# A third buffer for the first layer's raw weights, and one buffer fewer in two other places

## The chip, the cores and the metric

One core of a Trainium2 chip runs one program. A core has TensorE (PE; its weight loads are listed as PEld), VectorE (DVE), ScalarE (ACT), GpSimd (POOL) and SyncE (SP), which run their own instruction streams in order and wait for each other by semaphores, and 16 DMA engines that move data between the off-chip memory (HBM) and the on-chip memory (SBUF, 128 partitions). The metric is the device time of one execution in microseconds (us).

## The reference

Two residual branches, each behind a layer norm that a conditioning vector shifts and scales. 2048 tokens of 576 channels.

```python
sa, ca, ga, sb, cb, gb = ...            # (silu(c) @ w_mod), six vectors of 576
h = layernorm(x) * (1 + ca) + sa
x = x + ga * A(h)
h = layernorm(x) * (1 + cb) + sb
x = x + gb * B(h)

def A(u):                               # a long convolution over the tokens, per channel
    dt = exp(log_dt)
    P = exp((-exp(log_A_real) + 1j * A_imag) * dt * pos)      # 576 x 128 x 2048
    K = 2 * einsum("dn,dnl->dl", C * dt, P).real              # the kernel, 576 x 2048
    y = irfft(rfft(K, 4096) * rfft(u, 4096))[:2048]
    return y + u * D_skip

def B(x):                               # 576 -> 4608 -> 576
    return relu(x @ w1) @ w2
```

All data is float32.

## The kernel before

**The token blocks.** The 2048 tokens are worked in NB = 4 blocks of 512. For block s the convolution `conv(s)` makes the block's new x, its second layer norm and, by transposes, the operand tiles xh, xl and xs of the two-layer net; then 36 groups (NF = 36) of 128 hidden channels run for that block in `ffn`. So g counts 144 groups, block g // 36. To keep float32 accuracy with the rounded type that TensorE multiplies fast, each operand is split into a high and a low part; a product is made of three matmuls (high x high, high x low, low x high).

**One group of the net.** `first(g)` is 14 matmuls of w1's tile with xh, xl and xs into the PSUM tile hps (line 1326). ScalarE makes hh = relu(hps) (line 1331), DVE the low part hl (line 1332). `second(g)` is 14 matmuls of hh and hl with w2's tile into five accumulators (line 1352). In program order `second(g-1)` stands after `first(g)`.

**Where its weights come from.** The raw tiles are r1 (128 x 640, of w1, 320 KB) and r2 (128 x 576, of w2, 288 KB); both have the program's name r in the profile. They are loaded from HBM by SyncE's queue (lines 1271 and 1275), with two buffers for r1 and three for r2, and asked for three groups ahead: `load_r1(g + 3)`, `load_r2(g + 3)` at the head of group g's turn. ScalarE copies them to the rounded high part (`hi1`, line 1291; `hi2`, line 1301). In block 0 DVE subtracts to get the low parts (`lo1`, line 1296; `lo2`, lines 1307 and 1308), and SyncE's queue stores these to HBM (L1d, L2d, line 1408); in blocks 1 to 3 they are loaded back from there (lines 1280 and 1311), so r1 is then free again after the copy of line 1291. In block 0 it is free after the subtraction of line 1296. The tiles w1 and w2 have three buffers each. In the turn of group g, program order is: the loads, the stores of low parts, `first(g)`, `hi2(g+1)` and `lo2(g+1)`, `hi1(g+2)` and `lo1(g+2)`, `low1(g+3)`, `second(g-1)`.

**What runs between.** While the 36 groups of block b run, a generator does the work of the next block piece by piece: `step(g)` takes pieces until the block's rate is met (it counts the estimated DVE time that each piece yields). In block 0 this is `KGen.rest` for 12 sets of 48 channels (h), which makes the convolution kernel of later blocks, and then `conv(1)`. In block 1 it is the output of block 0 (`finish(0)`), `rest` again for h = 6 to 11, and `conv(2)`; in block 2 `finish(1)` and `conv(3)`; in block 3 `finish(2)`. What is left of a generator at the end of its block runs before the next block starts.

**`rest`.** For each h the tiles W0 (768 KB), Z (96 KB) and W2 (1536 KB) are loaded by POOL's queue, in program order (line 47 is the helper that keeps it; the tiles appear as W, Zr and W2r). A rotation (`rot`, lines 481 to 487) is four DVE operations; in block 1 the first of h reads W0 and makes the first half of W1, the second reads that half. `products` (line 515) multiplies W2 and W1 on TensorE, and ScalarE copies the result out (line 525). W0 and Z have three buffers, W2 two. The loads of W0 and Z for the second next h stand at the head of h's turn, that of W2 for the next h at its end.

**The convolution.** `product` multiplies spectra on DVE: a product into the tile T (line 1030), then a sum or difference with it (line 1032). T comes from `half`: two buffers in block 0's own convolution (ns = 6), three in those of blocks 1 to 3 (ns = 7).

**What sets the order.** A list scheduler orders the instructions of each engine by the program's order and by its own estimates of when things are ready; instructions wrapped in `Kept` or `keep_in_program_order` stay in program order. A tile that takes a buffer waits for the buffer's last readers. Pools are opened on two sides of SBUF, and the pools of the convolutions and of `rest` reuse each other's space one after the other.

Of the kernel before, what the change touches and what calls it, by code (L numbers as in the profile page):

```python
# [10 lines left out]
F32 = mybir.dt.float32  # L11
# [7 lines left out]
P = 128  # L19
# [8 lines left out]
H = 48  # L28
NH = 12
PC = 288  # L30
# [19 lines left out]
class KGen:  # L50
# [10 lines left out]
    def v(self, out, a, b, op):  # L61
        self.tc.keep_in_program_order(self.nc.vector.tensor_tensor(out, a, b, op=op))  # L62
# [391 lines left out]
    def rest(self, psum, plan):  # L454

        nc, k = self.nc, self.k
        v = nc.vector.tensor_tensor
        hs = list(plan)
        with ExitStack() as ctx:
            pt = k.pool(ctx, f"kr{len(hs)}", side="right")  # L460
            d = Kept(k.tc, nc.gpsimd).dma_start

            def load0(h):
                W0 = pt.tile([P, 2, H, 16], F32, tag="W0", bufs=3, name=f"W0_{h}")
                Z = pt.tile([P, 2, 2, H], F32, tag="Z", bufs=3, name=f"Zr_{h}")
                d(out=W0.rearrange("p r c a -> p (r c a)"), in_=k.W1d[h])
                d(out=Z.rearrange("p i r c -> p (i r c)"), in_=k.Zd[h])
                return W0, Z

            def load2(h):  # L470
                W2 = pt.tile([P, 2, H, 32], F32, tag="W2", bufs=2, name=f"W2r_{h}")
                d(out=W2.rearrange("p r c b -> p (r c b)"), in_=k.W2d[h])
                return W2

            def rot(out, X, Z, i):
                T = pt.tile([P, 2, H, 16], F32, tag="T", name="T")
                zr, zi = (
                    Z[:, i, r].unsqueeze(1).unsqueeze(3).broadcast_to([P, 2, H, 16])
                    for r in range(2)
                )  # L480
                v(T, X, zi, op=ALU.mult)  # L481
                yield 1.75
                v(out, X, zr, op=ALU.mult)  # L483
                yield 1.75
                v(out[:, 0], out[:, 0], T[:, 1], op=ALU.subtract)  # L485
                yield 0.95
                v(out[:, 1], out[:, 1], T[:, 0], op=ALU.add)  # L487
                yield 0.95

            def rots(h, W1, W0, Z):  # L490
                blocks = plan[h]
                a = [W1[:, :, :, 16 * i : 16 * i + 16] for i in range(len(blocks))]
                if blocks[0] == 1:
                    yield from rot(a[0], W0, Z, 0)
                    if len(blocks) > 1:
                        yield from rot(a[1], W0, Z, 1)
                        yield from rot(a[2], a[0], Z, 1)
                else:
                    yield from rot(a[0], W0, Z, 1)
                    yield from rot(a[1], a[0], Z, 0)  # L500

            ke = {}

            def products(h, W1, W2):
                blocks = plan[h]
                na = 16 * len(blocks)
                if h % 6 == 0:
                    ke[h // 6] = pt.tile([P, na, 72], F32, tag=f"ke{na}", bufs=1, name=f"ker_{h}")
                for half in range(2):
                    ps = psum.tile([P, 6, na], F32, tag="cps", bufs=1, name="kps")  # L510
                    for q in range(6):
                        for dd in range(4):
                            ch = dd * 12 + 6 * half + q
                            for r in range(2):
                                nc.tensor.matmul(  # L515
                                    ps[32 * dd : 32 * dd + 32, q, :],
                                    W2[:, r, ch],
                                    W1[:, r, ch],
                                    start=(r == 0),
                                    stop=(r == 1),  # L520
                                )
                        if q == 2:
                            yield None
                    q0 = 12 * (h % 6) + 6 * half
                    nc.scalar.activation(  # L525
                        ke[h // 6][:, :, q0 : q0 + 6], ps.rearrange("p q a -> p a q"), AF.Copy
                    )
                    yield None
                if h % 6 == 5:
                    yield -1  # L530
                    for i, s in enumerate(blocks):
                        self.store(
                            s, h // 6, ke[h // 6][:, 16 * i : 16 * i + 16].rearrange("p a q -> p (a q)"),
                            nc.sync,
                        )

            nxt = [load0(hs[0])]
            W2 = load2(hs[0])
            nxt.append(load0(hs[1]))
            for _ in range(1 if len(hs) == NH else 7):  # L540
                yield -1
            prev = iter(())
            for i, h in enumerate(hs):
                W0, Z = nxt.pop(0)
                if i + 2 < len(hs):
                    nxt.append(load0(hs[i + 2]))
                na = 16 * len(plan[h])
                bufs = 1 if len(plan[h]) != len(plan[hs[i - 1]]) else 2
                W1 = pt.tile([P, 2, H, na], F32, tag=f"W1{na}", bufs=bufs, name=f"W1r_{h}")
                yield from spread(rots(h, W1, W0, Z), prev, len(plan[h]))  # L550
                prev = products(h, W1, W2)
                if i + 1 < len(hs):
                    W2 = load2(hs[i + 1])
            yield from prev


def spread(a, b, n):

    for i, w in enumerate(a):
        yield w  # L560
        if i % n == n - 1:
            yield next(b, 0.0)
    yield from b


class Body:
# [259 lines left out]
        return self.cv.tile([P, 4, 2, PC], F32, tag="S", bufs=self.ns, name=name)  # L826

    def half(self, name):
        return self.cvl.tile([P, 4, PC], F32, tag="T", bufs=self.ns - 4, name=name)

    def load(self, src, name):
        t = self.spec(name)
# [426 lines left out]
    def ffn(self, gens):  # L1259

        nc, I, ff = self.nc, self.I, self.ff
        n = NB * NF
        r1, r2, w1, w2 = {}, {}, {}, {}
        late = []

        def queue(g):
            return Kept(self.tc, nc.sync) if g < 2 else nc.sync

        def load_r1(g):
            r1[g] = ff.tile([P, 5, P], F32, tag="r1", bufs=2, name="r1")  # L1270
            queue(g).dma_start(out=r1[g], in_=I["w1"][g % NF])

        def load_r2(g):
            r2[g] = ff.tile([P, D], F32, tag="r2", bufs=3, name="r2")
            queue(g + 1).dma_start(out=r2[g], in_=I["w2"][(g % NF) * P : (g % NF) * P + P, :])
# [14 lines left out]
        def hi1(g):  # L1290
            copy(g - 1)(w1[g][:, 0], r1[g], AF.Copy)  # L1291
# [7 lines left out]
        def hi2(g):  # L1299
            w = w2[g] = ff.tile([P, 1152], F32R, tag="w2", bufs=3, name="w2")  # L1300
            copy(g)(w[:, 0:D], r2[g], AF.Copy)  # L1301

        def lo2(g):
            w, r = w2[g], r2.pop(g)
            if g < NF:
                v = vec(g)
                v(w[:, D:640], r[:, 512:D], w[:, 512:D], op=ALU.subtract)
                v(w[:, 640:], r[:, :512], w[:, :512], op=ALU.subtract)
                late.append((self.L2d[g], w[:, D:]))
            else:  # L1310
                nc.sync.dma_start(out=w[:, D:].bitcast(F32), in_=self.L2d[g % NF])
# [84 lines left out]
        yield  # L1396
        load_r2(1)
        load_r1(2)
        load_r2(2)
        prev = None  # L1400
        for g in range(n + 1):
            if g < n:
                if g + 3 < n:
                    load_r1(g + 3)
                if g + 3 < n:
                    load_r2(g + 3)
                for dst, src in late:
                    nc.sync.dma_start(out=dst, in_=src.bitcast(F32))
                late.clear()
                new = (g, *first(g))  # L1410
                if g + 1 < n:
                    hi2(g + 1)
                    lo2(g + 1)
                if g + 2 < n:
                    hi1(g + 2)
                    lo1(g + 2)
                if g + 3 < n:
                    low1(g + 3)
                step(g)
            if prev is not None:  # L1420
                second(*prev)
                if prev[0] % NF == NF - 1:
                    self.evacuate(prev[0] // NF)
            if g < n:
                prev = new
                step(g)
                if g % NF == NF - 1:
                    for _ in gens[g // NF]:
                        pass
                    done[0] = 0.0  # L1430
# [126 lines left out]
```

## Time and profile before

| | us |
|---|---|
| median of 3 runs (1337.91 to 1348.62) | 1338.05 |
| the profiled execution | 1346.28 |
| its span, first to last instruction | 1344.5 |
| PE busy | 1218.3 (91%) |
| DVE busy | 895.8 (67%) |
| ACT busy | 494.6 (37%) |
| mean granted TensorE clock | 0.934 |
| DMA, mean over the span | 257 GB/s |

Busy times are sums over the span; a matmul's end is modelled, so a busy PE is not PE at its peak. A row of a group reads: line, engine, operation, out<-in, size, count, then busy us and mean ns of one, then the engine's idle time just before these instructions and what ended most of it. A row in order of time reads: start in us, length in us, engine, line, operation, out<-in, and in brackets the idle time before it and what ended that. A row of the waits reads: who waited for whom, us in total, times, the longest. A row of a window reads: stretch and its length, the busy time (and count) of PE, PEld, DVE, ACT and POOL, the granted clock, the share of the DMA engines, GB/s.

### The profile page before, as it was taken

The numbers are of one execution on the slowest core, as the hardware profiler recorded it, in microseconds if no ns is written. First come the engines' busy times: TensorE is split into PE (matmuls) and PEld (weight loads), VectorE is DVE, ScalarE is ACT, GpSimd is POOL, SyncE is SP. The second block draws the span as 40 slices with busy tenths as digits, with TensorE's granted clock in tenths as the row PEclk, the third lists the DMA queues.
The fourth block names the chain that finished last, engine by engine and source line by source line (L and its number), as shares of the span: only waits on it lengthen the run. The fifth ranks groups of instructions, "written<-read, shape, count | busy, mean of one in ns | idle before, by whom it ended". The sixth has DMA issues, their size and how long they took to land.

```text
span 1344.5 us, 26011 instructions
## 1 busy us (share of the span) xinstructions
PE 1218.3 (91%) x10720; PEld 963.8 (72%) x10720; DVE 895.8 (67%) x1324; ACT 494.6 (37%) x863; POOL 162.5 (12%) x260
## 2 busy tenths in 40 slices
PE   4565686889989998999999999999999999999997
PEld 3344564667768676777777887887888888888885
DVE  5999978997995999768658995467996221111112
ACT  5688523222223422622234225433323352323331
POOL 0656501001100100011001000100000000000000
PEclk9556767999999998999999999999999999999998
DMA  8567972987878877698889995867996667666661
GB/s 269 218 231 291 307 272 80 346 298 273 320 279 288 297 247 290 206 400 322 281 276 339 346 357 160 275 219 271 349 392 189 176 178 230 193 197 199 199 177 53
DMA packets 122379, 345.85 MB, mean 257 GB/s; under 512 B 23916, under 2 KB 24212, under 8 KB 111508
## 3 DMA queue, kind: packets, MB, share of 16 engines
q1 hardware_dynamic: 105364, 226.96, 50.9%
q0 software_dynamic: 16384, 115.85, 23.0%
q8 instruction: 84, 1.38, 0.4%
q10 hardware_dynamic: 512, 1.38, 0.3%
q14 instruction: 35, 0.29, 0.1%
HBM read 262.73 MB, written 81.40 MB: 256 GB/s over the span
## 4 chain that ended last, share of the span: by engine, by line
PE 72%; DVE 14%; DMA 7%; issue 4%; ACT 2%; POOL 1%; ACTq 0%; POOLq 0%; DVEq 0%; SPq 0%
PE acc L1352 29%; PE hps L1326 28%; DMA r<-in_w_dram 4%; PE ps_f L846 4%; PE kps L71 2%; PE ph L71 2%; PE kps L515 2%; PE ps_i L1053 2%; DVE W1r L483 2%; DVE T L481 2%; DMA L2d<-w 1%; DVE W1r L487 1%; DVE W1r L485 1%; DVE T L62 1%; DVE w L1296 1%
## 5 line engine op out<-in xcount | busy, mean ns | idle before, releaser
L1326 PE MATMUL hps<-xh,w 128*128 128x512 f32 x1152 | 393.6, 402 | 1.9 <-issue 1.1
L1352 PE MATMUL acc<-w,hh 128*128 128x512 f32 x1152 | 370.6, 403 | 12.9 <-ACT hh L1331 12.9
L1332 DVE SCALAR_TENSOR_TENSOR hl<-hps,hh 128x512 fp32r<-128x512 f32 x144 | 99.1, 688 | 310.1 <-ACT hh L1331 309.3
L1352 PEld LDWEIGHTS acc<-w,hh 128*128 128x128 f32 x1152 | 216.3, 189 | 60.7 <-ACT hh L1331 14.5
L1326 PEld LDWEIGHTS hps<-xh,w 128*128 128x128 f32 x1152 | 218.5, 190 | 50.2 <-issue 1.6
L1326 PE MATMUL hps<-xl,w 128*128 128x512 f32 x576 | 229.7, 400 | 0.1
L1352 PE MATMUL acc<-w,hl 128*128 128x512 f32 x576 | 223.0, 399 | 0.9 <-DVE hl L1332 0.9
L1331 ACT ACTIVATE hh<-hps 128x512 fp32r<-128x512 f32 x144 | 85.8, 596 | 289.7 <-PE hps L1326 289.4
L1301 ACT ACTIVATE w<-r 128x576 fp32r<-128x576 f32 x141 | 96.7, 686 | 231.0 <-PE acc L1352 219.5
L1291 ACT ACTIVATE w<-r 128x640 fp32r<-128x640 f32 x140 | 102.7, 733 | 92.8 <-DMA r<-in_w_dram 92.8
L1326 PEld LDWEIGHTS hps<-xl,w 128*128 128x128 f32 x576 | 109.3, 190 | 23.9 <-DVE xl L47 0.6
L1352 PEld LDWEIGHTS acc<-w,hl 128*128 128x128 f32 x576 | 107.9, 189 | 24.7 <-DVE hl L1332 2.1
L1326 PE MATMUL hps<-xs,w 128*128 128x512 f32 x288 | 98.6, 413 | 0.0
L71 PE MATMUL kps<-W,W 128*32 128x16 f32 x2304 | 39.9, 211 | 45.3 <-POOL W L68 28.1
L1032 DVE TENSOR_TENSOR Y<-Y,T 128x1152 f32<-128x1152 f32 x60 | 79.4, 1351 | 0.0
L71 PEld LDWEIGHTS kps<-W,W 128*32 128x32 f32 x2304 | 35.1, 144 | 59.0 <-POOL W L68 30.8
L847 ACT ACTIVATE Z<-ps_f 128x288 f32<-128x288 f32 x120 | 48.8, 408 | 70.2 <-PE ps_f L846 68.8
L515 PEld LDWEIGHTS kps<-W1r,W2r 128*32 128x32 f32 x3456 | 44.7, 113 | 37.7 <-issue 19.0
L515 PE MATMUL kps<-W1r,W2r 128*32 128x48 f32 (+2 forms) x3456 | 52.1, 201 | 14.6 <-ACT ker L525 9.3
L1471 POOL DMA_DIRECT2D out_dram<-x x16 | 8.7, 544 | 468.6 <-DVE x L1463 466.3
L1326 PEld LDWEIGHTS hps<-xs,w 128*128 128x128 f32 x288 | 54.0, 191 | 11.3
L1352 PE MATMUL acc<-hl,w 128*128 128x512 f32 x144 | 56.7, 394 | 0.0
(235 smaller groups left out, 1586.6 us busy)
## 6 DMA issues: line engine op xcount, KB each, us to landing
r<-in_w_dram SPq DMA_DIRECT2D x144, 320.0 KB, 7.3
r<-in_w_dram SPq DMA_DIRECT2D x144, 288.0 KB, 5.1
w<-L1d SPq DMA_DIRECT2D x108, 320.0 KB, 3.2
w<-L2d SPq DMA_DIRECT2D x108, 288.0 KB, 2.8
W2r<-W2d POOLq DMA_DIRECT2D x18, 1536.0 KB, 9.2
W2d<-W SPq DMA_DIRECT2D x12, 1536.0 KB, 8.6
Ua<-Ud POOLq DMA_DIRECT2D x15, 1152.0 KB, 9.6
W<-W1d POOLq DMA_DIRECT2D x18, 768.0 KB, 10.6
```

Of the source, the lines that this page charges most:

```text
L71: self.tc.keep_in_program_order(self.nc.tensor.matmul(*args, **kw))
L481: v(T, X, zi, op=ALU.mult)
L515: nc.tensor.matmul(ps[32 * dd : 32 * dd + 32, q, :], W2[:, r, ch], W1[:, r, ch], start=(r == 0), stop=(r == 1),)
L846: nc.tensor.matmul(o, fc[:, n2, c, :], src(n2), start=True, stop=True)
L847: ev = nc.scalar.activation(Z[:, n2, c], ps[:, :PC], AF.Copy)
L1032: v(y, y, T, op=op or ALU.add)
L1291: copy(g - 1)(w1[g][:, 0], r1[g], AF.Copy)
L1301: copy(g)(w[:, 0:D], r2[g], AF.Copy)
L1326: nc.tensor.matmul(ps, a, x, start=(i == 0), stop=(i == 13))
L1331: nc.scalar.activation(hh, ps, AF.Relu)
L1332: nc.vector.scalar_tensor_tensor(hl, ps, 0.0, hh, op0=ALU.max, op1=ALU.subtract)
L1352: nc.tensor.matmul(acc[i], a, x, start=(f == 0 and seen[i] == 1), stop=(f == NF - 1 and seen[i] == (3 if i < 4 else 2)),)
```

## The change

Three things:

- r1 gets a third buffer, and is asked for four groups ahead: `load_r1(3)` is added ahead of the loop, and in the loop `load_r1(g + 4)` takes the place of `load_r1(g + 3)`. r2 stays as it is.
- T has two buffers in all convolutions (three before in those of blocks 1 to 3).
- In block 1's `rest`, W0 has two buffers instead of three, and W0 and Z of h + 2 are asked for after the first rotation of h (`ahead`), in place of the head of h's turn. Block 0's `rest` keeps its three buffers and its place for the loads.

```diff
@@ KGen.rest
         hs = list(plan)
+        whole = len(hs) == NH
...
-                W0 = pt.tile([P, 2, H, 16], F32, tag="W0", bufs=3, name=f"W0_{h}")
+                W0 = pt.tile([P, 2, H, 16], F32, tag="W0", bufs=2 + whole, name=f"W0_{h}")
...
                     yield from rot(a[0], W0, Z, 1)
+                    ahead(h)
                     yield from rot(a[1], a[0], Z, 0)
...
+            def ahead(h):
+                if h + 2 in plan:
+                    nxt.append(load0(h + 2))
...
-            for _ in range(1 if len(hs) == NH else 7):
+            for _ in range(1 if whole else 7):
...
-                if i + 2 < len(hs):
+                if whole and i + 2 < NH:
                     nxt.append(load0(hs[i + 2]))
@@ Body.half
-        return self.cvl.tile([P, 4, PC], F32, tag="T", bufs=self.ns - 4, name=name)
+        return self.cvl.tile([P, 4, PC], F32, tag="T", bufs=2, name=name)
@@ Body.ffn
-            r1[g] = ff.tile([P, 5, P], F32, tag="r1", bufs=2, name="r1")
+            r1[g] = ff.tile([P, 5, P], F32, tag="r1", bufs=3, name="r1")
...
         load_r2(2)
+        load_r1(3)
         prev = None
         for g in range(n + 1):
             if g < n:
-                if g + 3 < n:
-                    load_r1(g + 3)
+                if g + 4 < n:
+                    load_r1(g + 4)
                 if g + 3 < n:
                     load_r2(g + 3)
```

## The prediction

> **What bounds the kernel now.** I read the page first: span, then the chain that ended last.
>
> ```profile
> span 1344.5 us, 26011 instructions
> PE 72%; DVE 14%; DMA 7%; issue 4%; ACT 2%; POOL 1%; ACTq 0%; POOLq 0%; DVEq 0%; SPq 0%
> L1291 ACT ACTIVATE w<-r 128x640 fp32r<-128x640 f32 x140 | 102.7, 733 | 92.8 <-DMA r<-in_w_dram 92.8
> ```
>
> TensorE carries 72% of the chain, and one row of the groups names what the change is about: the copy L1291, which makes the first layer's high half from the raw tile r1, left ScalarE idle for 92.8 us waiting for r1 to land. Whether that costs time depends on where it happens, so next the windows, cut near the changes of token block (block 0 from 236, where its first group is through, to 561; then 789 and 1011):
>
> ```profile
> 236.00:561.00 325.00, 299.39 (x3383) 230.82 (x3382) 284.82 (x381) 96.33 (x183) 24.64 (x44) 0.96 0.80 289
> 561.00:789.00 228.00, 224.09 (x2047) 177.08 (x2047) 174.77 (x209) 76.38 (x145) 24.83 (x43) 1.00 0.89 326
> 789.00:1011.00 222.00, 222.00 (x975) 179.49 (x974) 166.04 (x230) 84.65 (x155) 12.35 (x22) 1.00 0.79 277
> 1011.00:1344.50 333.50, 323.58 (x1442) 267.08 (x1440) 70.87 (x117) 105.83 (x171) 4.32 (x8) 0.99 0.61 179
> ```
>
> The columns are length, busy time of PE, weight loads, DVE, ACT and POOL, granted clock, DMA share and GB/s. From 561 on PE is busy in all but 14 us of 783: no load can be worth much there. Block 0 is the loose one: PE is idle for 25.6 us of 325 and DVE for 40.2, so both are nearly full and either can be the limit. Then the waits inside block 0, with those of SyncE's own queue behind them:
>
> ```profile
> ACT w L1291 <- DMA r<-in_w_dram: 82.6, 19, 11.2
> PE acc L1352 <- ACT hh L1331: 12.9, 3, 6.2
> PE kps L515 <- ACT ker L525: 5.3, 1, 5.3
> SPq L1275 <- DVE w L1308: 191.2, 27, 14.0
> SPq L1271 <- DVE w L1296: 14.8, 28, 3.4
> ```
>
> 82.6 of the 92.8 us lie here. How it reaches PE is seen in one stall in order of time:
>
> ```profile
> 277.09 0.33 SPq L1271 DMA_DIRECT2D r<-in_w_dram  x1
> 287.57 0.75 SPq L1271 DMA_DIRECT2D r<-in_w_dram  x1
> 297.51 0.74 ACT L1291 ACTIVATE w<-r 128x640 fp32r<-128x640 f32 x1 [8.82 <-DMA r<-in_w_dram]
> 298.16 0.24 ACT L525 ACTIVATE ker<-kps 128x96 f32<-128x96 f32 x1
> 298.45 0.48 PE L515 MATMUL kps<-W1r,W2r 128*32 128x16 f32 x18 [5.34 <-ACT ker L525]
> ```
>
> ScalarE works in order. The copy of group 9 waits 8.82 us for a tile asked for at 287.57; behind it stand the small copy L525 and the relu L1331, and PE needs one of these. The other stalls of PE that end with work queued behind that copy:
>
> ```profile
> 248.12 0.71 PE L1352 MATMUL acc<-w,hh 128*128 128x512 f32 x1 [2.14 <-ACT hh L1331]
> 401.28 0.79 PE L1352 MATMUL acc<-w,hh 128*128 128x512 f32 x1 [6.19 <-ACT hh L1331]
> 526.45 0.80 PE L1352 MATMUL acc<-w,hh 128*128 128x512 f32 x1 [4.53 <-ACT hh L1331]
> 604.24 0.56 PE L515 MATMUL kps<-W1r,W2r 128*32 128x32 f32 x36 [2.68 <-ACT ker L525]
> ```
>
> With the 5.34 above that is 20.9 us of idle PE, 18.2 of it in block 0. After four of them the clock is down:
>
> ```profile
> 248.20:251.60 3.40, 3.40 (x8) 2.65 (x9) 3.40 (x3) 0.69 (x1) 0.00 (x0) 0.50 0.97 401
> 298.45:302.80 4.35, 4.35 (x56) 3.60 (x57) 4.35 (x6) 0.43 (x1) 0.00 (x0) 0.50 0.90 353
> 401.28:405.20 3.92, 3.92 (x98) 3.05 (x99) 3.87 (x6) 1.05 (x3) 0.00 (x0) 0.50 0.08 29
> 526.45:531.50 5.05, 5.05 (x12) 3.99 (x13) 5.05 (x7) 1.25 (x2) 0.00 (x0) 0.50 0.11 45
> ```
>
> At clock 0.50 half of each stretch is lost: 1.7, 2.2, 2.0 and 2.5, together 8.4 us. PE's own loss to the wait is therefore 20.9 + 8.4 = 29.3 us. [...]
>
> **Third buffer for r1.** Before, r1(g+3) takes the tile of r1(g+1); after, r1(g+4) does. The event that frees it is the same (the subtraction L1296 of g+1 in block 0, the copy L1291 of g+1 later), so the request for each tile goes out where now the one before it goes out, and SyncE's queue keeps its shape: the SyncE rows show that L1275 (r2) waits long for L1308, and L1271 then only 0.5 us more. For group 9 the request moves from 287.57 to 277.09, 10.5 us against a wait of 8.82. The longest wait of all is 11.2, so I take nearly all of the 82.6 us as gone. One request of 320 KB moves out of the loop to ahead of it: at block 0's 289 GB/s that is 1.1 us of transfer. Bounds 0 to 1.1 us; I take nothing, since the loop's first copies have their tiles by then.
>
> What the stalls are worth is not PE's loss alone, because DVE is the limit in much of block 0. First its busy time (third pair of columns) over 123 us of it, then the waits of DVE that follow the stalls:
>
> ```profile
> 263.00:386.00 123.00, 112.30 (x2075) 86.88 (x2076) 115.83 (x123) 28.09 (x52) 12.63 (x24) 0.96 0.82 295
> ```
>
> ```profile
> 260.91 1.76 DVE L483 TENSOR_TENSOR W1r<-W,Zr 128x1536 f32<-128x1536 f32 x1 [2.43 <-PE kps L515]
> 322.92 1.76 DVE L483 TENSOR_TENSOR W1r<-W,Zr 128x1536 f32<-128x1536 f32 x1 [7.17 <-PE kps L515]
> 401.25 0.69 DVE L1332 SCALAR_TENSOR_TENSOR hl<-hps,hh 128x512 fp32r<-128x512 f32 x1 [2.51 <-ACT hh L1331]
> 410.61 0.69 DVE L1332 SCALAR_TENSOR_TENSOR hl<-hps,hh 128x512 fp32r<-128x512 f32 x1 [5.46 <-ACT hh L1331]
> 522.64 1.36 DVE L1030 TENSOR_TENSOR T<-Ka,Ua 128x1152 f32<-128x1152 f32 x1 [0.97 <-DMA Ua<-Ud]
> 543.96 0.46 DVE L1058 TENSOR_TENSOR x<-ps_i,x 128x288 f32<-128x288 f32 x1 [1.44 <-PE ps_i L1053]
> ```
>
> In those 123 us DVE is idle for 7.2, which is the wait of 7.17 at 322.92 and nothing else. For each stall I take the smaller of PE's loss and of DVE's wait that comes of it. First stall: PE 2.14 + 1.7 = 3.8, DVE 2.43: 2.4. Second: PE 5.34 + 2.2 = 7.5, DVE 7.17: 7.2. Third: PE 6.19 + 2.0 = 8.2, DVE 2.51 + 5.46 = 8.0: 8.0. Fourth: PE 4.53 + 2.5 = 7.0, DVE 0.97 + 1.44 = 2.4: 2.4. In block 1, where DVE has room, PE's 2.68: 2.7. Sum 22.7 us. Where the wait goes, the next late thing is the tile after it, which now has the old tile's place in the queue: it lands just when it is wanted, and that is why I take the smaller side each time.
>
> **Two product tiles (T).** The product L1030 and the sum L1032 that reads it are both on DVE, which works in order, so a tile fewer adds no wait on another engine; it can only force a sum to stand directly behind its own product. The nearest row for that is in the chain:
>
> ```profile
> 484.66 0.31 issue
> ```
>
> It is time in front of a sum L1032 for which nothing is named. A gain is out, since a buffer fewer lets nothing start earlier. The convolution in block 0 has 12 such pairs (2 and 4, for two halves): 0 to 12 x 0.31 = 3.7 us. I take the middle, 1.9. In blocks 1 and 2 DVE has 53 and 56 us of room and it costs nothing.
>
> **Two W0 tiles in block 1.** W0 of h+2 is now asked for when the first rotation of h has read W0 of h, no longer at the start of h, and its request stands in POOL's queue ahead of W2 of h+1.
>
> ```profile
> 576.35 0.53 POOL L47 DMA_DIRECT2D W<-W1d  x1 [1.50 <-DMA out_dram<-x]
> 584.38 1.75 DVE L483 TENSOR_TENSOR W1r<-W,Zr 128x1536 f32<-128x1536 f32 x1
> 605.42 1.76 DVE L481 TENSOR_TENSOR T<-W,Zr 128x1536 f32<-128x1536 f32 x1
> DMA to landing us min/median/max: 9.4/12.8/16.1
> 609.36 0.53 POOL L47 DMA_DIRECT2D W2r<-W2d  x1 [16.46 <-PE kps L515]
> ```
>
> The third W0 (h = 8) moves from 576.35 to 586.1, when L483 of h = 6 has read its tile; with the slowest landing of that stretch, 16.1, it is there at 602.2, and its first reader L481 is at 605.42. So 3.2 us are left over, and 2.7 for the small Z tile that goes out right behind it, one issue of 0.53 later. W2 of h = 7 now stands behind both, until 587.2, and at 16.1 again lands by 603.3; its products come after those of h = 6, which end at 609.36. Cost nothing, hidden by the rotations of h = 7; if that cover is gone DVE starts a rotation a few us late, and DVE has 53 us of room in this block. Bounds 0 to 3 us.
>
> **The sum.** 22.7 - 1.9 = 20.8 us off the profiled execution of 1346.3 us (span 1344.5 and 1.8 around it), 1325.5. That execution lies 8.2 us above the median of the runs shown, 1338.05, and inside their spread (1337.91 to 1348.62). I take the same difference off the median: 1317.
>
> **Rivals.** *PE gets it all:* the scheduler lets DVE work slide into the freed places, and the whole 29.3 us come back: 1309. For it: DVE idles 40.2 us in block 0. Against: the 123 us shown above, in which DVE has no idle time but the one wait.
>
> *The next wait takes over:* the following r1 tile, the stores of the low halves and DVE's own load eat half or more of it. For it: DVE is busy 284.8 of 325 us, so in a block 0 shortened by 20 us it would be at 93%; and each next tile lands when the stalled one did, so a group that runs earlier can find it late in its turn. Then a third to a half of 22.7 remains, 7 to 11 us: 1327 to 1331, about 1329.
>
> *The tiles land no earlier:* if the DMA engines were full, asking earlier would only move the waiting into the queue: 1338. For it: shares of 0.97 and 0.90 in two of the slow stretches. Against: 0.80 over block 0, and 0.08 and 0.11 right behind the other two stalls, when nothing was asked for. [...]
>
> *Slower, by ScalarE's order:* with r1 there a group earlier, the list scheduler puts the copy L1291 in front of the relu of the same group also in blocks 1 and 2, where it now stands behind it:
>
> ```profile
> 740.21 0.60 ACT L1331 ACTIVATE hh<-hps 128x512 fp32r<-128x512 f32 x1 [2.49 <-PE hps L1326]
> 740.70 0.73 ACT L1291 ACTIVATE w<-r 128x640 fp32r<-128x640 f32 x1
> ```
>
> Each of these 72 groups would get its relu up to 0.73 us late, 52.6 us at most. It makes the kernel over 1% slower once 20.8 + 13.4 = 34.2 us of that are really lost, that is 47 of 72 groups in full; all of them give 1338 - 20.8 + 52.6 = 1370. Against: what lets L1291 go at 740.70 is the same end of the first layer that lets the relu go, since the w1 tile has three buffers and not r1; and there is room before PE needs the relu.
>
> **How the numbers follow.** Forecast 0.46, with its own range from 1311 (the fourth stall at PE's 7.0 instead of 2.4 and no cost of T: 27.3) to 1323 (T at 3.7, W0 at 3, the extra request at 1.1: 14.9); PE gets it all 0.08; next wait takes over 0.26; no earlier landing 0.07; slower 0.13. The likeliest is the forecast, 1317. The range takes in all but the slower case: from 1308, the whole of PE's loss, to 1340, no gain and the 1.9 us of T. That holds 0.87; without the case of no gain it would hold exactly 0.80 and end at 1331, which leaves the take-over case no room for the upper ends of the costs, so I leave it in. About 1% (13.4 us) is what a measurement of this kernel can tell from no change. Faster by more: 0.46 + 0.08 = 0.54; within: 0.26 + 0.07 = 0.33; slower: 0.13.
>
> **What would show it.** In the profile after: L1291's idle time on r1 under 15 us; the stalls of PE behind ScalarE in block 0 gone, and with them most of the stretches at clock 0.50; block 0 some 300 to 306 us long, DVE busy over 93% of it; blocks 1 to 3 unchanged to 3 us; in block 1 no DVE wait on W0. I am wrong if r1's wait is gone and block 0 stays above 318 us: then DVE or another transfer was the limit all along. I am wrong in the mechanism if r1's wait stays.

## The result, and the profile after

The kernel after takes 1332.58 us (median of 20 runs, 1329.04 to 1340.35), the kernel before, run beside it on the same chips, 1342.51 us (20 runs, 1337.91 to 1351.3). The ratio is 0.9932, with a 95% interval from 0.9916 to 0.9947: 0.7% or about 9 us faster, where 20.8 us (1.6%) were forecast. It is inside the 1% that was called no change. The profiled execution has a span of 1331.4 us, against 1344.5 before. Of these 13.1 us, 8.6 lie in block 0 and 2.1 in block 1; the other 2.5 lie ahead of group 0, whose start varies from 223.3 to 229.1 us over all profiles of this document.

From the page of the kernel after, its span and the row of the copy of the first layer's high half (L1291 before, L1297 now):

```profile
span 1331.4 us, 25993 instructions
L1297 ACT ACTIVATE w<-r 128x640 fp32r<-128x640 f32 x140 | 102.6, 733 | 59.1 <-DMA L1d<-w 53.8
```

The wait for r1 is gone to the last microsecond. In its place the same copy waits 53.8 us for something else: the landing of `L1d<-w`, the store of the low half of a w1 tile. That tile has three buffers; the copy of group g+3 writes into the one whose low half group g has stored, and may not start before the store has read it. Next, the waits within block 0 (from the first matmul of group 0 to that of group 36, 224.80 to 548.70; columns: us in total, times, longest), and above them the row of the window:

```profile
224.80:548.70 323.90, 304.02 (x3404) 233.98 (x3405) 291.92 (x393) 100.00 (x189) 27.83 (x50) 0.97 0.81 291
ACT w L1297 <- DMA L1d<-w: 53.8, 11, 11.3
PE kps L517 <- ACT ker L527: 8.1, 3, 4.7
PE kps L517 <- issue: 5.7, 5, 2.0
PE acc L1358 <- ACT hh L1337: 3.2, 2, 2.8
DVE hl L1338 <- ACT hh L1337: 20.0, 9, 8.3
SPq L1281 <- DVE w L1314: 178.4, 26, 12.0
```

The same cut of the kernel before:

```profile
227.30:559.80 332.50, 306.78 (x3405) 236.62 (x3406) 292.16 (x393) 100.25 (x189) 27.79 (x50) 0.95 0.79 283
PE acc L1352 <- ACT hh L1331: 12.9, 3, 6.2
PE kps L515 <- ACT ker L525: 5.3, 1, 5.3
PE kps L515 <- issue: 5.0, 4, 2.4
```

Block 0 went from 332.5 to 323.9 us. It was forecast at 300 to 306 for a slightly different cut of 325.0, that is 19 to 25 us shorter, where the terms of the sum that lie in block 0 give 18.1. Taken off that cut, the 8.6 us leave about 316, just under the 318 that was named as the sign of being wrong. TensorE's stalls behind ScalarE (the PE rows that name ACT) went from 18.2 to 11.3 us, not to nothing. Ahead of each of the four of over 1 us (1.61, 1.79, 4.70 and 2.77) the copy has just waited for that store, 2.9, 2.7, 7.0 and 11.3 us. One of them, in order of time:

```profile
378.09 0.33 SPq L1277 DMA_DIRECT2D r<-in_w_dram  x1
378.48 0.96 SPq L1415 DMA_DIRECT2D L2d<-w  x1
379.49 1.77 SPq L1415 DMA_DIRECT2D L1d<-w  x1
...
393.29 0.74 ACT L1297 ACTIVATE w<-r 128x640 fp32r<-128x640 f32 x1 [6.99 <-DMA L1d<-w]
394.50 0.41 ACT L527 ACTIVATE ker<-kps 128x288 f32<-128x288 f32 x1
...
394.96 1.29 PE L517 MATMUL kps<-W1r,W2r 128*32 128x48 f32 x52 [4.70 <-ACT ker L527]
```

The store's way from issue to landing in this stretch:

```profile
DMA to landing us min/median/max: 13.7/13.7/13.7
```

So the store of 379.49 landed at 393.2, and the copy of three groups later started at 393.29. The stall comes at nearly the same place as that of 401.28 in the kernel before, and is 4.70 instead of 6.19 us long. There the copy for group 19 held up the relu; here the copy for group 20 holds up the second layer's copy and the small copy L527. The clock still falls at four places in block 0, for 17.0 us together instead of 31.1:

```profile
394.00:400.80 6.80, 5.84 (x105) 4.81 (x105) 0.09 (x1) 1.34 (x4) 0.00 (x0) 0.50 0.33 131
516.90:520.30 3.40, 3.40 (x10) 2.66 (x9) 3.40 (x4) 1.31 (x2) 0.00 (x0) 0.50 0.38 146
281.30:284.70 3.40, 3.40 (x100) 2.53 (x92) 3.40 (x6) 1.17 (x2) 0.00 (x0) 0.51 0.00 1
346.20:349.60 3.40, 3.05 (x19) 2.48 (x19) 3.40 (x5) 0.00 (x0) 0.00 (x0) 0.50 1.01 317
```

### The profile page after: what moved, and what is told of

It is laid out like the page before. It is cut to its first block, busy times and chain, and to the rows that moved or that the text cites. A ratio compares the mean times of both kernels' runs of the same rounds, so it can differ in the third digit from the quotient of the medians.

```text
span 1331.4 us, 25993 instructions
## 1 busy us (share of the span) xinstructions
PE 1209.0 (91%) x10720; PEld 956.7 (72%) x10720; DVE 895.4 (67%) x1324; ACT 494.5 (37%) x863; POOL 162.8 (12%) x260
## 3 DMA queue, kind: packets, MB, share of 16 engines
q0 software_dynamic: 16384, 115.85, 23.1%
q8 instruction: 84, 1.38, 0.4%
q10 hardware_dynamic: 512, 1.38, 0.3%
## 4 chain that ended last, share of the span: by engine, by line
PE 68%; DVE 17%; DMA 7%; issue 4%; ACT 2%; POOL 1%; SPq 0%; ACTq 0%; DVEq 0%; POOLq 0%
PE acc L1358 28%; PE hps L1332 27%; PE ps_f L852 5%; DMA L1d<-w 3%; PE kps L71 2%; PE ph L71 2%; DVE T L482 2%; DVE W1r L484 2%; PE ps_i L1059 2%; PE kps L517 1%; DVE w L1302 1%; DVE W1r L486 1%; DVE W1r L488 1%; DVE w L1314 1%; DVE T L62 1%
## 5 line engine op out<-in xcount | busy, mean ns | idle before, releaser
L1358 PE MATMUL acc<-w,hh 128*128 128x512 f32 x1152 | 366.4, 400 | 3.3 <-ACT hh L1337 3.2
L1297 ACT ACTIVATE w<-r 128x640 fp32r<-128x640 f32 x140 | 102.6, 733 | 59.1 <-DMA L1d<-w 53.8
L853 ACT ACTIVATE Z<-ps_f 128x288 f32<-128x288 f32 x120 | 49.0, 410 | 70.5 <-PE ps_f L852 68.5
L1358 PE MATMUL acc<-hh,w 128*128 128x512 f32 x144 | 57.5, 399 | 0.0
```

What stands on the lines that cost most here:

```text
L853: ev = nc.scalar.activation(Z[:, n2, c], ps[:, :PC], AF.Copy)
L1358: nc.tensor.matmul(acc[i], a, x, start=(f == 0 and seen[i] == 1), stop=(f == NF - 1 and seen[i] == (3 if i < 4 else 2)),)
```

## The experiments

Three theories of where the other 11 us are. The *store theory* (S in the first expectations): the store's landing now holds the copy, and takes back most of what r1's wait cost. The *order theory* (O): what counts is that a waiting copy stands ahead of the relu on ScalarE. The *VectorE theory* (V): block 0 is set by VectorE, so TensorE's stalls were never worth what they last. Three more came up on the way: full DMA engines (traffic), the supply of TensorE's instructions, and TensorE's own work as the limit.

**The small tiles alone.** The kernel after with r1 at two buffers, asked for three groups ahead, as before:

```
-            r1[g] = ff.tile([P, 5, P], F32, tag="r1", bufs=3, name="r1")
+            r1[g] = ff.tile([P, 5, P], F32, tag="r1", bufs=2, name="r1")
-        load_r1(3)
-                if g + 4 < n:
-                    load_r1(g + 4)
+                if g + 3 < n:
+                    load_r1(g + 3)
```

> The changed kernel with r1 back at two buffers and three groups ahead: only the two smaller pools (T, W0) are left of the change. Theory S (the store of a w1 tile's low half now limits the copy L1297), theory O (the relu stands behind a waiting copy on ScalarE, whatever the copy waits for) and theory V (VectorE is the limit of block 0) all expect the time of the kernel before, ratio 0.997 to 1.003, with the copy's wait for r1 again at 85 to 100 us. If the smaller pools cost what the prediction allowed them (up to 3.7 + 3 us) the ratio is 1.002 to 1.005; then the third buffer alone would be worth more than the whole change shows.

Measured: ratio 0.9987, interval 0.9961 to 1.0014. The two smaller tiles cost nothing that can be seen, and the gain is r1's. The order of the instructions on each engine is that of the kernel before, and yet the copy's wait for r1 in block 0 is 60.9 us and not 82.6: so much does this wait differ between two executions of one order.

```profile
ACT w L1297 <- DMA r<-in_w_dram: 60.9, 16, 11.4
```

**The tile w1 in two parts,** three buffers for its high half and four for its low half, so that the copy no longer waits for the store:

```
-            w = w1[g] = ff.tile([P, 2, 5, P], F32R, tag="w1", bufs=3, name="w1")
+            w = w1[g] = [ff.tile([P, 5, P], F32R, tag=f"w1{x}", bufs=dict(h=3, l=4)[x], name="w1") for x in "hl"]
```

> The changed kernel with the w1 tile as two tiles, the high half with three buffers and the low half with four, so that the copy into the high half need not wait until the low half's store has landed. Theory S: the copy's wait for the store (53.8 us) falls under 10 us, the two stalls of PE behind ScalarE in block 0 go, ratio to the kernel before 0.983 to 0.988 (the change alone: 0.993). Theory V: the wait falls as well, but block 0 gets shorter by at most 3 us, ratio 0.990 to 0.994. Theory O: like S, as long as nothing else takes the copy's wait.

Measured: 0.9979 (0.9953 to 1.0005), slower than the kernel after. The store's wait is gone, but two others stand in its place:

```profile
ACT w L1297 <- PE hps L1332: 54.1, 19, 7.4
ACT w L1297 <- DMA r<-in_w_dram: 36.3, 6, 10.2
PE kps L517 <- issue: 13.5, 6, 3.2
PE acc L1358 <- ACT hh L1337: 8.7, 3, 4.3
```

The expectation of the store theory missed. The edit was no clean test, since r1 came late again; why it did is open.

**ScalarE in the written order,** all through block 0, on the kernel after and on the one before:

```
-            return (Kept(self.tc, nc.scalar) if g < 3 else nc.scalar).activation
+            return (Kept(self.tc, nc.scalar) if g < NF else nc.scalar).activation
-            nc.scalar.activation(hh, ps, AF.Relu)
+            copy(g)(hh, ps, AF.Relu)
```

> The changed kernel with the relu and the two copies of each group of block 0 held in program order on ScalarE, so that the relu of group g stands ahead of the copies for groups g+1 and g+2; buffers and loads as in the changed kernel. Theory O: the copy still waits for the store (30 us or more in all), but no PE stall behind ScalarE of over 1.5 us is left in block 0, ratio 0.983 to 0.989. Theory S: the first layer of group g+2 waits for its tile instead of the second layer waiting for its relu, ratio 0.991 to 0.995. Theory V: 0.990 to 0.995.

> The kernel before, with two buffers for r1, and the same order held on ScalarE in block 0. Theory O: the wait for r1 stays (60 us or more) but costs PE little, ratio 0.986 to 0.993, as good as the change or better. Theory S and the prediction's own step (the tile's landing is what costs the time): ratio 0.997 to 1.002, since every tile lands as late as before.

Measured: 1.0052 (1.0021 to 1.0084) and 1.0079 (1.0064 to 1.0094), both slower than before. And yet the copies hardly wait any more: on the kernel after not at all for the store, on the kernel before 5.8 us in block 0 for raw tiles, with two buffers for r1. That was in no expectation, and it shows that a wait of ScalarE is not yet time. On the kernel after, group 20 starts at 406.4 us instead of 413.2; but groups 20 to 24 take 50.0 us instead of 36.1 and groups 32 to 36 45.7 instead of 36.1. In the first of these two stretches TensorE waits 4.0 us for the convolution's copies (L853), where the kernel after has no such wait, and the clock is 0.90 instead of 1.00. That these copies then stand behind the layer's is the likely reason, not shown by itself. So the order was kept for groups 0 to 18 alone (`g < 19` in the lines above), and the stores were tried ahead of the loads in SyncE's queue, each alone and both together:

```
             if g < n:
+                for dst, src in late:
+                    nc.sync.dma_start(out=dst, in_=src.bitcast(F32))
+                late.clear()
                 if g + 4 < n:
                     load_r1(g + 4)
                 if g + 3 < n:
                     load_r2(g + 3)
-                for dst, src in late:
-                    nc.sync.dma_start(out=dst, in_=src.bitcast(F32))
-                late.clear()
```

> The kernel after, with the stores of the two low halves put in SyncE's queue ahead of the two loads of the group instead of behind them; TensorE's order is the same to the instruction, and the other engines' nearly so. Store theory (the first layer's copy now waits for the landing of the low half's store, and this wait is what ate the forecast gain): the copy's wait for the store falls from 53.8 us to under 20, the TensorE stalls at 395 (4.70 us) and 516 (2.77 us) go, and the time is about 8 us below the kernel after: ratio to before 0.987. VectorE theory (block 0 is set by VectorE, busy 172.6 of the 188.4 us up to group 20): the wait falls, and the time stays within 2 us of the kernel after: ratio 0.993. Third possibility: the raw tiles, now behind the stores, land later and take the stores' place: wait moves to r1, ratio 0.993 to 0.997.

> The kernel after, with ScalarE's relu and weight copies kept in the written order for groups 0 to 18 only, the part before the convolution. Order theory (a copy that waits stands ahead of the relu): the gain that the order kept over all of block 0 had up to group 20 (406.4 against 413.2 us, 6.8 us) stays, and the losses of groups 20 to 24 and 32 to 36 do not come: about 1326, ratio to before 0.988. VectorE theory: no gain, 0.993.

> Both edits, stores first and ScalarE's order kept for groups 0 to 18. Store and order theories together: the copy no longer waits and nothing stands behind it, up to 12 us below the kernel after: ratio 0.984. VectorE theory: 0.993. If the two cure the same stall, the result is that of the better one alone.

Measured: stores first 0.9889 (0.9858 to 0.9921), order in part 0.9935 (0.9910 to 0.9959), both 0.9908 (0.9875 to 0.9940). The order theory gives nothing: in part, the order has group 20 start at 414.5 us, no sooner than the kernel after, so the 6.8 us above are not shown to be the order's. Stores first does what it says: the copy's wait for the store, 53.8 us, is gone. (How much sooner the stores land is not shown, since the trace has the landing of only one of them.) But r1, now behind the stores, is late 33.4 us, and TensorE finds another wait:

```profile
ACT w L1297 <- DMA r<-in_w_dram: 33.4, 9, 9.0
PE kps L517 <- issue: 10.8, 7, 3.4
PE acc L1358 <- ACT hh L1337: 1.9, 1, 1.9
PE kps L517 <- ACT ker L527: 1.5, 1, 1.5
```

A fourth buffer for r1 on top, asked for five groups ahead, takes the copy's wait for r1 away and is no better, as the supply theory had it: 0.9913 (0.9876 to 0.9949).

> Stores first, and a fourth buffer for r1, asked for five groups ahead. Stores first alone still had 40.2 us of waiting for r1 in block 0 and 5 stalls of TensorE that end in the supply of instructions. Store theory: r1's wait goes, the copy waits for neither, and up to 4 us more come off: ratio to before 0.986. Supply theory (TensorE's remaining stalls are in its instruction blocks, which come through the same DMA engines as the loads): no TensorE stall was left behind that wait, so nothing changes: 0.989.

**Is an engine the limit?** VectorE's last addition of each rotation left out, and one of TensorE's fourteen matmuls of the first layer left out (the low part of one of the four 128-row tiles of the model width, not of the tokens as the expectation says):

```
-                v(out[:, 1], out[:, 1], T[:, 0], op=ALU.add)
```

```
+            if 2 < g < NF:
+                ops.pop(-2)
```

> The kernel after without the last addition of each rotation (24 of 0.947 us in block 0, 22.7 us of VectorE; the computation lacks the imaginary part's second term). VectorE theory: block 0 (first group to group 36, 323.9 us) gets at least 15 us shorter, near 1312 in all. Store and order theories: what PE waits for is not VectorE, block 0 loses less than 6 us, about 1327.

> The kernel after with one matmul fewer of the first layer's fourteen in groups 3 to 35 of block 0 (the low part of one of the four token tiles left out): 33 x 0.412 = 13.6 us less for TensorE, VectorE's work unchanged. TensorE theory (block 0 is TensorE's work plus its stalls): block 0 falls by 10 to 14 us from 323.9. VectorE theory: by less than 4 us.

Measured, the windows of block 0 (less VectorE first, less TensorE second):

```profile
223.77:549.55 325.78, 304.99 (x3404) 236.46 (x3405) 272.15 (x369) 99.77 (x189) 27.84 (x50) 0.96 0.81 290
```

```profile
224.26:545.32 321.06, 299.08 (x3373) 230.28 (x3374) 292.02 (x393) 100.42 (x189) 27.78 (x50) 0.96 0.82 294
```

With VectorE 19.8 us less busy (291.92 to 272.15) block 0 is 1.9 us longer, not 15 shorter, and the ratio is 0.9936 (0.9909 to 0.9963), that of the kernel after. The VectorE theory falls. (TensorE's order changes in places too, since the scheduler orders anew, so this is a test of the limit and not of single stalls.) Less TensorE gives 2.8 us of block 0 and 0.9957 (0.9922 to 0.9991). The expectation of 13.6 us was priced wrongly: it took the mean duration of a matmul, 0.412 us, but they overlap and start 0.23 us apart in the median of the kernel after. Two of its rows show the overlap,

```profile
340.90 0.40 PE L1358 MATMUL acc<-w,hh 128*128 128x512 f32 x1
341.14 0.40 PE L1358 MATMUL acc<-w,hl 128*128 128x512 f32 x1
```

so the 33 are worth about 7.6 us. Of these, 4.8 do not show in the length of block 0: TensorE's idle time there rose from 19.9 to 22.0 us, and its time at half clock from 17.1 to 24.4.

**Traffic.** The stores left out but for groups 0 and 1, on the kernel after and on the one before:

```
-                late.append((self.L1d[g], w[:, 1].rearrange("p k c -> p (k c)")))
+                if g < 2:
+                    late.append((self.L1d[g], w[:, 1].rearrange("p k c -> p (k c)")))
-                    ... in_=self.L1d[g % NF]
+                    ... in_=self.L1d[g % 2]
```

and the same for L2d. The later blocks then read the low halves of groups 0 and 1 in place of all.

> The kernel after without the stores of the low halves, but for groups 0 and 1, whose rows the later blocks then read in place of all (the low halves of the other groups are wrong; the bytes loaded are the same). Block 0 moves some 20 MB less. Store theory: as with stores first or better, the copy waits for no store: 0.987. Supply theory: with the DMA share in block 0 down from 0.83 to about 0.6, the instruction blocks come in time, the 5.7 us of unnamed waits at the small products fall under 3, and block 0 falls from 323.9 to about 312: ratio 0.982.

> The kernel before without the same stores. If the r1 wait of before comes from full DMA engines, it falls from 82.6 us to under 30 without a third buffer, and the time comes near that of the kernel after without stores (0.984). If it comes from the late request alone, the wait stays above 60 us and the ratio above 0.99.

Measured: 0.9891 (0.9858 to 0.9925) and 0.9948 (0.9916 to 0.9979).

```profile
223.43:537.07 313.64, 301.27 (x3405) 231.94 (x3405) 291.69 (x393) 100.20 (x189) 27.87 (x50) 0.98 0.65 234
PE kps L517 <- issue: 7.0, 6, 2.9
```

```profile
225.20:547.20 322.00, 305.04 (x3405) 235.67 (x3406) 292.21 (x393) 100.64 (x189) 27.77 (x50) 0.97 0.63 228
ACT w L1291 <- DMA r<-in_w_dram: 65.8, 17, 9.1
```

The first two rows are of the kernel after without stores, the last two of the kernel before without them. Even with a DMA share of 0.63 r1 is late with two buffers, and as late as in the small tiles alone (60.9 us): its wait is the late request more than full engines, which was the forecast's reading. And the wait of the products that nothing is named for stays, at 7.0 us, with a share of 0.65; less traffic does not take it away, and that part of the supply theory missed.

**The store's wait taken away in kernels that compute everything,** beside the kernel after and stores first once more. The first layer's low half is subtracted anew in every block, neither stored nor loaded:

```
-            if g < NF:
-                vec(g)(w[:, 1], r, w[:, 0], op=ALU.subtract)
-                late.append((self.L1d[g], w[:, 1].rearrange("p k c -> p (k c)")))
+            vec(g)(w[:, 1], r, w[:, 0], op=ALU.subtract)
```

with the load of `L1d` in `low1` gone; or the second layer's (`lo2`), in the same way, with stores first.

> The kernel after unchanged, beside the others: ratio to before 0.993, and the copy's wait for the store's landing in block 0 again near 50 us.

> Stores first, the same kernel as before. Store theory: 4 to 6 us below the kernel after in the same session. If the wait for the store costs nothing: within 2 us of it.

> The first layer's low half is subtracted anew in every block (108 more subtractions of 0.815 us on VectorE, 88 us over blocks 1 to 3) and neither stored nor loaded. Store theory: the wait of 53.8 us is gone in block 0 with its 11.3 us of TensorE stalls behind ScalarE, block 0 falls from 323.9 to 313 to 317. In blocks 1 and 2 VectorE goes from 181 to 210 of 233 us and from 165 to 194 of 221: no cost if it fits, 5 to 15 us if it does not. Ratio 0.985 to 0.990.

> Stores first, and the second layer's low half subtracted anew in every block instead of stored and loaded (10.6 MB less to move in block 0; 0.9 us more of VectorE for each group later). Traffic theory: instruction blocks and tiles come earlier, block 0 falls below the 321.3 us of stores first, to about 317: ratio 0.985. Store theory: the first layer's store is what counts, and it is already early; no gain over stores first: 0.989.

Measured: 0.9929 (0.9904 to 0.9954), 0.9921 (0.9894 to 0.9949), 0.9886 (0.9854 to 0.9918) and 0.9900 (0.9872 to 0.9928). Beside each other, stores first is 0.75 us below the kernel after (medians 1330.51 and 1331.26; ten runs from 1325.59 to 1338.32): its first result, from four runs, was in part luck, and what moving the store is worth cannot be told. Taking it away is worth 5.8 us by the medians (1325.43). A profile alone would have misled here: in that of stores first again block 0 is 317.4 us, no longer than with the low half recomputed (318.1), but group 0 starts at 229.1 us and not at 223.5. The kernel without the second layer's stores has the shortest block 0 of those that compute everything, 315.9 us, as the traffic theory had it, and a time of 0.9900, as the store theory had it; it decides nothing between them.

Block 0 with the first layer's low half recomputed:

```profile
223.49:541.58 318.09, 303.13 (x3405) 233.66 (x3406) 293.99 (x396) 100.54 (x189) 27.87 (x50) 0.98 0.73 259
PE kps L517 <- issue: 9.6, 7, 2.8
PE acc L1351 <- DVE hl L1331: 2.5, 2, 1.5
```

No wait behind ScalarE is left among TensorE's larger ones, and the products' unnamed wait is longer instead. Two last runs, the same kernel again and with the second layer's stores first:

> The same kernel as f3: ratio 0.988 to 0.990; TensorE's waits at the small products (behind ScalarE and for instructions together) again 8 to 12 us, the relu's wait under 2 us.

> First layer's low half recomputed, and the second layer's stores ahead of the loads. If tiles still decide: ratio 0.985. If what is left in block 0 is the small products' own waits: the same as g1, 0.988 to 0.990.

Measured: 0.9897 (0.9871 to 0.9922) and 0.9876 (0.9847 to 0.9905). The second has the lowest ratio of all: its interval lies wholly below that of the kernel after in the result above, though the two were not run beside each other. In the profile of the first the unnamed waits are 7.0 us, and at the very matmul of the 4.70 us stall shown above TensorE idles 3.22 us once more, this time because the copy waits 5.8 us for r1. So that place stalls when any of the copy's tiles is late.

## Why the prediction was wrong

**How much of block 0 the losses explain.** For each kernel the stalls of TensorE in block 0, in us: behind the relu (acc waits for hh), at the small products behind ScalarE (kps waits for ker) and for nothing named, all its idle time, and the sum of the stretches at half clock. All gaps count, so that a figure can lie a little above its row of the waits, which leave out the shortest. The last column is block 0 without the idle time and half of those stretches.

| kernel | block 0 | relu | products, ScalarE | products, unnamed | all idle | half clock | rest |
|---|---|---|---|---|---|---|---|
| before | 332.4 | 12.9 | 5.3 | 5.1 | 25.7 | 31.1 | 291.2 |
| after | 323.9 | 3.2 | 8.1 | 5.7 | 19.9 | 17.1 | 295.5 |
| after again | 323.7 | 3.1 | 10.9 | 4.9 | 21.3 | 13.8 | 295.5 |
| stores first | 321.2 | 1.9 | 1.5 | 10.8 | 19.5 | 10.2 | 296.6 |
| stores first again | 317.4 | 1.8 | 5.1 | 4.8 | 15.1 | 14.4 | 295.2 |
| no stores | 313.6 | 0.0 | 0.0 | 7.1 | 12.4 | 10.2 | 296.1 |
| low half recomputed | 318.1 | 0.5 | 0.2 | 9.9 | 15.0 | 13.8 | 296.2 |
| less VectorE | 325.8 | 0.0 | 7.2 | 11.4 | 20.8 | 27.3 | 291.4 |
| less TensorE | 321.1 | 3.8 | 5.2 | 7.2 | 22.0 | 24.4 | 286.9 |

The rest is 291 to 297 everywhere but in the last row, which has 7.6 us of work less. Idle time inside the half-clock stretches counts twice in it; counted once, the rest is 293.1 to 296.8, and 287.7 in the last row. So block 0 is TensorE's work and what it loses, and a stall taken away is time won where no other takes its place. What the forecast had wrong is which of them go.

**Point by point.** *The tile arrives in time:* right, 82.6 us of waiting for r1 to none.

*"The next late thing is the tile after it ... it lands just when it is wanted":* this step failed. The next late thing was the store of the low half, which holds the w1 tile: 53.8 us in 11 waits. It stands last of four requests in SyncE's queue, all let go by VectorE's subtractions of one turn; of the 15 stores in block 0 whose landing the trace has, the middle one took 6.9 us to land. The rival "the next wait takes over" named these stores and priced itself at 7 to 11 us; about 9 came. What the store holds back is seen in the kernels without it: about 5 us of the time (5.8 beside the kernel after), not the whole 11 to 12 that are missing. These kernels also move less, so the buffer and the traffic are not told apart: in the kernels that only change the buffer or the queue (w1 in two parts, stores first) r1 is late in the store's place.

*The second stall at 7.2 us:* this term was mis-sized. Its 5.34 us lie at the small products, and those wait in any case. Behind ScalarE and unnamed together they idle 10.4 us before, 13.8 after, and 7 to 16 in every kernel of the table but the one with less VectorE (18.6). Where ScalarE is no longer late the unnamed wait is mostly the larger of the two. The part that could be won is the relu's 12.9, of which 9.7 were.

*The third stall at 8.0 us:* the profiles give next to nothing for it. From the start of group 8 to that of group 28 the kernel before took 185.7 us and the one after 184.8; the store's 13.7 us to its landing put the stall back (4.70 us, with 6.80 us at half clock; 2.31 us in the second profile of the same kernel).

*The first and the fourth:* up to group 8 the change won 5.1 us, where 9.6 were due with the second; from 28 to 36 it won 2.6 for a forecast of 2.4. The second profile of the kernel after gives 3.6 up to group 8, 2.9 from 8 to 28 and 2.3 from 28 to 36, so single figures here are good to about 2 us. *Block 1:* 2.1 us from group 36 to 72 for a forecast of 2.7; but 1.3 longer than before in the second profile (284.6 against 283.3 us), so the forecast is not shown to be met.

*The smaller of TensorE's loss and VectorE's wait:* a wrong reason. VectorE's 88% before and 90% after did not set block 0: with 19.8 us less of it nothing got shorter. It did little harm to the second and third, whose two sides lay within 0.3 us of each other. In the fourth (7.0 against 2.4) the smaller side came near the 2.6 us that were won, which is luck, since the reason for taking it is gone.

*T at 1.9 us:* nothing that can be seen (0.9987 for both smaller tiles, the same order on every engine); the interval ends at 1.0014, which is 1.9 us, so a cost of that size lies at the edge of what the runs allow. *W0 at nothing:* right; the only wait of VectorE for a load of the rotations in block 1 is that for Zr, 9.6 us, and 9.1 before.

*Slower by ScalarE's order:* it did not happen; blocks 1 to 3 kept their length to 2.1 us in the profile after. Its premise was misread. The copy shown at 740.70, behind the relu of group 57, is the one for group 60; the copy for two groups on had already run ahead of the relu in the kernel before, in all 106 groups from 36 to 141, and does so after in the same 106. In block 0 it stood ahead in 29 of the groups 4 to 35 before and stands so in 31 after. With the order turned round, all through block 0 or in part, nothing was won.

*The base:* 1338.05 was the median of three runs. With 20 it is 1342.51, so the forecast stood 4.5 us too low from the start.

About 4 us of the 20.8 are not accounted for even in the best kernel (0.9876, about 16.6 us): the unnamed waits at the products are there in all of the table, and what sets their length is open.

## What to carry to other kernels

When a late load is moved forward, follow the buffer on the other side of the instruction that waited for it: the copy needed both a full r1 and a free w1, and the profile names only the later of the two. Before a stall is added to a sum, look whether the same place also idles in groups where nothing was late; such a place has a second wait under the first. And one execution is a thin base: two kernels with one order differed by 22 us in the wait that this change was about.

## What the runs showed of the hardware

The unnamed waits come at fixed places of the program: in three kernels TensorE stops after 35 of the same 48 products of 16 columns, for 1.72, 3.20 and 2.80 us. Here the kernel with stores first, around one of them, and then what the DMA engines did in the stretch from 346.40 to 347.55:

```profile
343.90 1.10 PE L517 MATMUL kps<-W1r,W2r 128*32 128x16 f32 x94
344.93 0.73 PE L1332 MATMUL hps<-xh,w 128*128 128x512 f32 x2
345.60 0.52 PE L517 MATMUL kps<-W1r,W2r 128*32 128x16 f32 x35
348.92 0.33 PE L517 MATMUL kps<-W1r,W2r 128*32 128x16 f32 x13 [2.80 <-issue]
```

```profile
q0 software_dynamic: 81, 0.43, 92.3%
q8 instruction: 1, 0.02, 5.2%
```

The stall begins at 346.12, one packet of instructions is moved inside it (346.50 to 347.46), and the matmuls go on about 1.5 us after its end. TensorE had just run 94 products, with a weight load each, in 1.10 us. A second sign comes from numbering TensorE's matmuls and weight loads in the order in which they start. Block 0 has 79 unnamed stops of over 0.7 us in the twenty profiles; 76 of them lie 193 or 194 places behind a multiple of 256, and the matmuls go on 1.1 to 1.6 us after the end of a packet of 16384 bytes on the instruction queue. The page of the kernel before has 84 packets on that queue (1.38 MB) for 21440 matmuls and weight loads, 255 to a packet. So the likeliest reading, an estimate from these numbers, is that such a packet brings TensorE its next 256 or so instructions (the "instruction blocks" of the expectations), and that TensorE had used up those it had before the next were there. It was not tested by itself, since no kernel here changes their supply. In block 0 of the kernel after 27 such packets are moved, and three unnamed stops of over 0.7 us stand beside them; why some packets come late and others do not is open. If the reading holds, late packets may be behind the 5 to 11 us of unnamed waits at the products in the table above.
